# An adaLN attention block on one core: a third row tile is moved behind the first K row, and the scale is made in other parts

## The chip, the core and the metric

The kernel runs on one core of a Trainium2 chip. The core has a matrix engine (PE in the profile, its weight loads PEld), a vector engine (VectorE, DVE), an activation engine (ScalarE, ACT), a general engine (GpSimd, POOL) and a sequencer that issues most transfers (SyncE, SP). The metric is the device time of one execution, in microseconds (us), lower is better. The kernel before took 96.18 us (median of 3 runs, 95.69 to 96.2).

## What is computed

```python
B, N, D = (2, 256, 1152)
mod = (silu(c) @ w_mod).reshape(B, 6, 1, D)
shift_a, scale_a, gate_a = mod[:, 0], mod[:, 1], mod[:, 2]
h = layernorm(x) * (1 + scale_a) + shift_a
q, k, v = split(h @ wqkv, 3)
p = softmax(einsum('bqd,bkd->bqk', q, k) * D ** -0.5)
return x + gate_a * (einsum('bqk,bkd->bqd', p, v) @ wo)
```

All inputs are bfloat16. D is 9 blocks of 128; the 512 token rows (B times N) are 4 row tiles of 128, two for each batch item.

## The kernel before

**How the work is staged.** The row tiles of x are centred, transposed on the matrix engine into `xcT` (9 blocks of D by 512 tokens), and multiplied by 1 + scale block by block, which gives `hTs`. K is made from `hTs` at once, without the layernorm's 1/std, which is multiplied into the scores later, and without the shift, which adds the same to all scores of a query. In the meantime the 1/std of all tokens is made (`rstd_bc`), `normalised` multiplies it into `hTs` to give `hT`, and `shifted` adds the shift. Q and V are made from `hT`, then the scores, softmax, p times V, and the output product.

**K by rows.** K has 9 output blocks f and is summed over 9 blocks k of D, one `wK` row of 288 KB for each k. Five output blocks (NACC) are summed in five PSUM banks (`accs`, the pool MM) as the rows arrive: `k_part(k, tokens)` for the blocks 0 and 1 of D (the part PA; KA is 2), a piece of the tokens at a time, and `k_step(k)` for the rest, with all 512 tokens in one matmul of 128x512 each. For the other four output blocks, the share of the D blocks 0 and 1 is made by `pair` and `pair_part` into a bank `psE` and copied to SBUF by `park` (the `held` tile); the D blocks 2 to 8 are summed by `held_block(i, rows)` in a bank `psK`, and `add_held(i)` adds both.

**Three more PSUM banks.** BA, BB and BC are pools of one bank each. A tile that is put there waits until the one before it in the same bank has been read. Junk matmuls (`fillers`), the transposed tiles `tp`, the scale `psS`, the shift `psH`, `psE`, `psK`, `pT3` and `bc_ps` take turns in them.

**The scale.** `psS` is silu(c) times the scale columns of `w_mod` (`wS`). There are two ways to make it. `scale_rows` uses 128x128 blocks of `wS` as weights and 32 columns of silu(c) as moving operand, 9 matmuls for each block; the result lies as it is needed, and `scale_out` adds 1. `scale_tiles` uses silu(c) as 32 columns of weights in four column tiles of the array and streams `wS`, 36 matmuls for a part; `scale_turned` transposes the result on VectorE (`sT`) and adds 1. The blocks come in the parts PA (2 blocks), PB (3), PC (2) and PD (2). PB is made by `scale_tiles`, the others by `scale_rows`. The shift is made by `shift_tiles` the same way as `scale_tiles`, for all 9 blocks.

**Order.** Every engine's instructions run in the order in which the program records them (`pin`), SP's transfers too. So where a line stands in the code is where its instruction stands on its engine. Transfers go out on SP in the order of L167 to L192 and L532 to L539.

**Lines that the change touches.** The loads L172 to L192; `fillers` L362; the start of the K stage L372 to L419 (tile 2 is transposed at L385 and L386, ahead of the first K row at L395); part PB and the second pairs L420 to L437; the K rows with the parts PC and PD, L453 to L487; the shift L505 to L523. From L557 on (Q, scores, V, output) nothing changes but the line numbers.

Of the kernel before, what the change touches and what calls it, by code (L numbers as in the profile page):

```python
# [16 lines left out]
def kernel(  # L17
# [10 lines left out]
    P = 128  # L28
# [9 lines left out]

    NACC = 5
    NPARK = KT - NACC  # L40
    PA, PB, PC, PD = (0, 2), (2, 5), (5, 7), (7, KT)
    KA = PA[1]
    NR = 32

# [21 lines left out]
    def bank(shape, name, dtype=None, where=None):  # L66
        if where is None:
            where = ring[turn_no[0] % len(ring)]
            turn_no[0] += 1
        return where[0].tile(shape, dtype or F32, tag=where[1], name=name)  # L70
# [36 lines left out]
    def tok(b):  # L107
        return slice(b * N, (b + 1) * N)

    def one(t):  # L110
        return slice(t * P, (t + 1) * P)
# [42 lines left out]
    def load_s(part, k0, k1):  # L154
        load_mod(wS, 1, k0, k1, part[0] * P, part[1] * P)

    def load_k(k0, k1, c0=0, c1=D):
        spq.dma_start(out=wK[:, k0:k1, c0:c1], in_=wqkv_v[:, k0:k1, D + c0 : D + c1])
# [19 lines left out]
    load_s(PB, 4, KT)  # L178
    load_k(2, 3)
    load_k(3, 4)  # L180
    load_k(4, 5)
    load_s(PC, 0, 4)
    load_s(PC, 4, KT)
    load_k(5, 6)
    load_s(PD, 0, 4)
    load_s(PD, 4, KT)
    load_k(6, 7)
    load_k(7, KT)
    for k0, k1 in ((0, 3), (3, 6), (6, KT)):
        load_mod(wH, 0, k0, k1, 0, D)  # L190
    for k0, k1 in ((0, 2), (2, 5), (5, 7)):
        load_q(k0, k1)  # L192

    junk_ps = bank([P, 512], "junk_ps", where=BB)
# [1 line left out]
    def fillers(n):  # L196
        for _ in range(n):
            ten.matmul(junk_ps, lhsT=junk[:, :P], rhs=junk, start=True, stop=True)
# [44 lines left out]
    def centre(t, scalar, op, c0=0, c1=D):  # L243
        vec.tensor_scalar(out=xc[:, t, c0:c1], in0=x_sb[:, t, c0:c1], scalar1=scalar, scalar2=None, op0=op)
# [4 lines left out]
    def transposes(t, h, where):  # L249
        k0, k1 = HALF[h]  # L250
        tp = bank([P, 5, P], "tp", BF16, where)
        for k in range(k0, k1):
            ten.transpose(tp[:, k - k0, :], xc[:, t, k * P : (k + 1) * P], ident)
        tps[t, h] = tp

    def xcT_copy(t, h, on_dve, skip=0):
        k0, k1 = HALF[h]
        dst, srct = xcT[:, k0 + skip : k1, one(t)], tps[t, h][:, skip : k1 - k0, :]
        if on_dve:
            vec.tensor_copy(out=dst, in_=srct)  # L260
        else:
            sca.copy(out=dst, in_=srct)
# [16 lines left out]
    def scale_rows(part, kk0, kk1, js=None, where=None):  # L279
        opened = part == PA  # L280
        if kk0 == 0 and not opened:
            psS[part] = bank([P, part[1] - part[0], NR], "psS", where=where)
        for j0, j1 in [part] if js is None else js:
            for kk in range(kk0, kk1):
                for j in range(j0, j1):
                    ten.matmul(psS[part][:, j - part[0], :], lhsT=wS[:, kk, j * P : (j + 1) * P], rhs=sc_rhs(kk),
                               start=(kk == 0 and j == part[0] and not opened), stop=(kk == KT - 1),
                               skip_group_check=True)
# [5 lines left out]
    wS_v = wS.rearrange("p kk (k j c) -> p kk k j c", k=KT, j=4)  # L294
    sT = const.tile([P, KT, 32], F32)

    def scale_tiles(part, where):
        psS[part] = bank([P, part[1] - part[0], 32], "psS", where=where)
        for kk in range(KT):
            for j in range(4):  # L300
                ten.matmul(psS[part][32 * j : 32 * j + 32], lhsT=sc_rhs(kk), rhs=wS_v[:, kk, part[0] : part[1], j, :],
                           start=(kk == 0), stop=(kk == KT - 1))

    def scale_turned(part):
        vec.transpose(out=sT[:, part[0] : part[1], :].rearrange("p k c -> p (k c)"),
                      in_=psS[part].rearrange("p k c -> p (k c)"))
        vec.tensor_scalar_add(out=s1p[:, part[0] : part[1], :], in0=sT[:, part[0] : part[1], 0:B], scalar1=1.0)
# [4 lines left out]
    def scaled_tp(k, t):  # L312
        vec.tensor_scalar(out=hTs[:, k, one(t)], in0=tps[t, 0][:, k, :], scalar1=s1p[:, k, t // NQ : t // NQ + 1],
                          scalar2=None, op0=ALU.mult)

    def scaled_b(k, b):
        scaled(k, tok(b), s1p[:, k, b : b + 1])
# [4 lines left out]
    def k_part(k, sl):  # L322
        for f in range(NACC):
            ten.matmul(accs[f][:, sl], lhsT=wk(k, f), rhs=hTs[:, k, sl],
                       start=(k == 0 and sl.start == 0), stop=False, skip_group_check=True)

    def pair(i, b, where):
        return bank([P, 2, N], "psE", where=where), NACC + 2 * i, tok(b)

    def pair_part(pr, k):  # L330
        ps, f0, sl = pr
        for i in range(2):
            ten.matmul(ps[:, i, :], lhsT=wk(k, f0 + i), rhs=hTs[:, k, sl],
                       start=(k == 0 and i == 0), stop=(k == KA - 1), skip_group_check=True)
# [6 lines left out]
    def park(pr, on_dve=False):  # L341
        ps, f0, sl = pr
        evac(on_dve, held[:, f0 - NACC : f0 - NACC + 2, sl], ps)

    def k_step(k, f0=0, f1=NACC):
        for f in range(f0, f1):
            ten.matmul(accs[f], lhsT=wk(k, f), rhs=hTs[:, k, :],
                       start=False, stop=(k == KT - 1), skip_group_check=True)
# [10 lines left out]
        vec.tensor_tensor(out=qkT[:, KT + NACC + i, :], in0=psK[i], in1=held[:, i, :], op=ALU.add)  # L359


    fillers(11)  # L362
    scale_open(PA, BA)
    sca.activation(out=e_sb, in_=c_sb, func=ACT.Exp, scale=-1.0)
    gps.tensor_scalar_add(out=e_sb, in0=e_sb, scalar1=1.0)
# [7 lines left out]
    transposes(0, 1, MM)  # L373
    xcT_copy(0, 0, True)
    xcT_copy(0, 1, False)
    transposes(1, 0, MM)
    transposes(1, 1, MM)
    scale_rows(PA, 0, 4)
    centre(2, nmean[:, 2:3], ALU.add)
    xcT_copy(1, 0, True)  # L380
    xcT_copy(1, 1, False)
    scale_rows(PA, 4, KT, js=[(0, 1), (1, 2)])
    scaled(0, tok(0), psS[PA][:, 0, 0:1])
    vec.tensor_copy(out=s1p[:, PA[0] : PA[1], :], in_=psS[PA][:, :, 0:B])
    transposes(2, 0, BB)  # L385
    transposes(2, 1, BC)  # L386
    scaled_tp(0, 2)
    scaled_b(1, 0)
    scaled_tp(1, 2)
    xcT_copy(2, 0, True, skip=KA)  # L390
    xcT_copy(2, 1, False)


    accs = [bank([P, T], "acc", where=MM) for _ in range(NACC)]
    k_part(0, tok(0))  # L395
    k_part(0, one(2))
    pr10 = pair(0, 0, BC)
    pair_part(pr10, 0)
    H3, C3 = 5 * P, 4 * P
    sca.activation(out=xc[:, 3, 0:H3], in_=x_sb[:, 3, 0:H3], func=ACT.Copy, accum_out=ssum[3])  # L400
    half3 = small.tile([P, 1], F32, tag="half3", name="half3")
    vec.reduce_sum(out=half3, in_=x_sb[:, 3, H3:D], axis=AX.X)
    vec.tensor_scalar(out=nmean[:, 3:4], in0=half3, scalar1=ssum[3], scalar2=-1.0 / D, op0=ALU.add, op1=ALU.mult)
    centre(3, nmean[:, 3:4], ALU.add, 0, C3)
    centre(3, nmean[:, 3:4], ALU.add, C3, D)
    k_part(1, tok(0))
    pair_part(pr10, 1)
    k_part(1, one(2))
    pr20 = pair(1, 0, BA)
    park(pr10)  # L410
    pair_part(pr20, 0)
    transposes(3, 0, BB)
    pair_part(pr20, 1)
    transposes(3, 1, BC)
    scaled_tp(0, 3)
    scaled_tp(1, 3)
    xcT_copy(3, 0, True, skip=KA)
# [2 lines left out]
    st3 = small.tile([P, NCH, 6], F32, tag="stats", name="stats")  # L420
    bn_part(3, st3, 0)
    act_var(1)
    k_part(0, one(3))
    scale_tiles(PB, BB)
    k_part(1, one(3))
    scale_turned(PB)
    for k in range(*PB):
        for b in range(B):
            scaled_b(k, b)
    bn_part(3, st3, 1)  # L430
    bn_part(3, st3, 2)
    vec.bn_aggr(out=mvs[:, 3, :], in_=st3)
    pr11, pr21 = pair(0, 1, BA), pair(1, 1, BC)
    for pr in (pr11, pr21):
        for k in range(KA):
            pair_part(pr, k)
        park(pr, on_dve=(pr is pr21))  # L437
    act_var(2)
    parts_sq = const.tile([P, P], BF16)
    gps.memset(parts_sq, 0.0)  # L440
# [16 lines left out]
            for b in range(B):  # L457
                scaled_b(k, b)

    for k in range(*PB):  # L460
        k_step(k)
    held_block(0, (2, 4), BA)
    scale_part(PC)
    held_block(0, (4, 5))
    held_block(1, PB, BC)
    pT3 = bank([P, P], "pT3", BF16, BB)
    ten.transpose(pT3, parts_sq, ident)
    masked = const.tile([P, TT, P], BF16)
    vec.tensor_tensor(out=masked, in0=pT3.unsqueeze(1).to_broadcast([P, TT, P]), in1=mask, op=ALU.mult)
    k_step(5)  # L470
    scale_part(PD)
    k_step(6)
    bc_ps = bank([P, T], "bc_ps", where=BB)
    ten.matmul(bc_ps, lhsT=junk[:, :P], rhs=masked.rearrange("p t n -> p (t n)"), start=True, stop=True)
    held_block(0, PC)
    held_block(1, PC)
    sca.copy(out=rstd_bc, in_=bc_ps)

    def normalised(k):
        vec.tensor_tensor(out=hT[:, k, :], in0=hTs[:, k, :], in1=rstd_bc, op=ALU.mult)  # L480

    for k in range(*PD):
        k_step(k)
    for f in range(NACC):
        evac(False, qkT[:, KT + f, :], accs[f])
# [13 lines left out]
    def shift_tiles(kk0, kk1):  # L499
        for kk in range(kk0, kk1):  # L500
            for j in range(4):
                ten.matmul(psH[32 * j : 32 * j + 32], lhsT=sc_rhs(kk), rhs=wH_v[:, kk, :, j, :],
                           start=(kk == 0), stop=(kk == KT - 1))

    shift_tiles(0, KT)  # L505
    held_block(3, (KA, KT), BC)
    shT = const.tile([P, KT, 32], F32)
    vec.transpose(out=shT.rearrange("p k c -> p (k c)"), in_=psH.rearrange("p k c -> p (k c)"))

    def shifted(i):  # L510
        k, b = divmod(i, B)
        if i % 3 == 2:
            sca.activation(out=hT[:, k, tok(b)], in_=hT[:, k, tok(b)], func=ACT.Identity,
                           bias=shT[:, k, b : b + 1], scale=1.0)
        else:
            vec.tensor_scalar(out=hT[:, k, tok(b)], in0=hT[:, k, tok(b)], scalar1=shT[:, k, b : b + 1],
                              scalar2=None, op0=ALU.add)

    for i in range(KT * B):
        if i in (3 * B, 5 * B):  # L520
            normalised(KT - 2 if i == 3 * B else KT - 1)
        shifted(i)
# [215 lines left out]
```

## Time and profile before

| | us |
|---|---|
| median of 3 runs (lowest, highest) | 96.18 (95.69, 96.2) |
| the profiled execution's own time | 95.85 |
| span of its trace, first to last instruction | 94.1 |
| matrix engine busy | 88.4 (94%) |
| VectorE busy | 70.1 (74%) |
| ScalarE busy | 34.3 (36%) |
| GpSimd busy | 21.1 (22%) |
| granted matrix clock, whole span | 1.00 |

The span is smaller than the execution's time by what lies ahead of the first and behind the last instruction. A busy time counts an instruction from its start to its end; matmuls overlap, and their ends are modelled, so for the matrix engine it is safer to look at the distance between starts: 0.216 us for a 128x512 matmul, 0.109 for 128x256, 0.056 for 128x128, 0.025 for 128x32. All recorded helpers share one line number, L85, so an instruction is told apart by the tiles that it writes and reads: `acc<-hTs,wK` is a K row, `psE` a pair, `psK` a held block, `psQ` the Q product, and `ps` the V, p times V and output products. A row of the timeline merges equal instructions that follow each other on one engine: start, duration, engine, operation, tiles, shape, count, and in square brackets the idle time ahead of it and what ended it.

### The profile page before, as it was taken

What the parts mean: (1) busy time and instruction counts of PE and PEld (TensorE: products, weight loads), DVE (VectorE), ACT (ScalarE), POOL (GpSimd) and SP (SyncE); (2) the same over time, 40 slices, a digit from 0 to 9 for tenths busy, and PEclk for the clock granted to TensorE, in tenths of its full rate; (3) what the DMA queues carried; (4) which work ended last, traced back from release to release, by engine and by line L of the source; (5) the groups of instructions that cost most, each with busy time, mean ns of one, the idle gap of its engine ahead of it and who ended that gap; (6) DMA issues with size and microseconds to landing.
All of it is one profiled execution on the core that took longest, in us unless ns stands there. A gap on an engine that the chain in (4) does not pass through costs nothing.

```text
span 94.1 us, 1693 instructions
## 1 busy us (share of the span) xinstructions
PE 88.4 (94%) x664; PEld 52.6 (56%) x664; DVE 70.1 (74%) x133; ACT 34.3 (36%) x71; POOL 21.1 (22%) x26
## 2 busy tenths in 40 slices
PE   3967999999999999999999999999999999999970
PEld 1346885554445444444469656565679656565660
DVE  2396979256899968999998899990028587889880
ACT  5199789002554600184320688324246300000010
POOL 5623000810000000000000000008999990002000
DMA  2999999999999999999999602200000000302213
GB/s 30 331 302 385 374 394 362 373 410 409 403 409 408 412 409 414 397 373 365 382 412 412 254 8 56 61 2 0 0 0 0 0 0 7 125 37 88 109 47 95
DMA packets 17216, 21.31 MB, mean 226 GB/s; under 512 B 2233, under 2 KB 10553, under 8 KB 17209
## 3 DMA queue, kind: packets, MB, share of 16 engines
q1 hardware_dynamic: 16793, 21.17, 62.0%
q8 instruction: 5, 0.08, 0.4%
q10 hardware_dynamic: 416, 0.04, 0.3%
q14 instruction: 2, 0.02, 0.0%
HBM read 19.76 MB, written 1.18 MB: 223 GB/s over the span
## 4 chain that ended last, share of the span: by engine, by line
PE 84%; DVE 4%; DMA 4%; ACT 2%; SPq 1%; issue 1%; DVEq 0%; ACTq 0%
PE ps L85 39%; PE psQ L85 19%; PE acc L85 11%; PE psK L85 7%; DMA x_sb<-in_x_dram 4%; PE s_ps L85 4%; PE psE L85 2%; DVE o_sb L85 2%; DVE ga L85 2%; PE psS L85 1%; ACT xc L85 1%; SPq L85 1%; PE psH L85 1%; PE tp L85 1%; DVE xc L85 1%
## 5 line engine op out<-in xcount | busy, mean ns | idle before, releaser
L85 POOL PARTITION_ALL_REDUCE gate_bc<-gacc x2 | 13.7, 6886 | 44.6 <-DVE gacc L85 44.6
L85 DVE SCALAR_TENSOR_TENSOR gacc<-wG,scT_f,gacc 128x1152 f32<-128x1152 bf16 x16 | 22.4, 1416 | 0.4
L85 PE MATMUL ps<-wV,hT 128*128 128x384 bf16 x108 | 17.7, 326 | 0.0
L85 PE MATMUL psQ<-hT,wQ 128*128 128x512 bf16 x81 | 17.6, 379 | 0.0
L85 PE MATMUL ps<-wO,attnT 128*128 128x384 bf16 (+3 forms) x108 | 17.2, 322 | 0.0
L85 PEld LDWEIGHTS <-attnT 128*128 128x128 bf16 x117 | 11.1, 98 | 6.5
L85 PEld LDWEIGHTS <-hT 128*128 128x128 bf16 x108 | 10.6, 98 | 6.9
L85 PEld LDWEIGHTS <-wK 128*128 128x128 bf16 x109 | 9.5, 97 | 7.0 <-issue 0.4
L85 PEld LDWEIGHTS <-wQ 128*128 128x128 bf16 x81 | 7.9, 98 | 9.6
L85 PE MATMUL acc<-hTs,wK 128*128 128x512 bf16 (+2 forms) x65 | 11.2, 313 | 0.0
L85 ACT CAST qkT<-psQ 128x512 bf16<-128x512 f32 x9 | 4.9, 597 | 11.1 <-PE psQ L85 11.1
L85 DVE CAST attnT<-ps 128x512 bf16<-128x512 f32 (+1 forms) x6 | 3.5, 603 | 6.8 <-PE ps L85 6.8
L85 DVE TENSOR_TENSOR ga<-ps,gate_bc 128x384 f32<-128x384 f32 (+3 forms) x12 | 6.5, 545 | 2.8 <-PE ps L85 2.7
L85 ACT CAST v_sb<-ps 128x384 bf16<-128x384 f32 x12 | 5.5, 477 | 7.9 <-PE ps L85 7.9
L85 DVE TENSOR_TENSOR o_sb<-ga,x_sb 128x384 bf16<-128x384 f32 (+3 forms) x12 | 6.6, 547 | 0.4
L85 PE MATMUL psK<-hTs,wK 128*128 128x512 bf16 x28 | 6.9, 379 | 0.0
L85 ACT CAST o_sb<-ps 128x128 bf16<-128x128 f32 x1 | 0.3, 266 | 17.3 <-PE ps L85 17.3
L85 DVE TENSOR_TENSOR hT<-hTs,held 128x512 bf16<-128x512 bf16 x9 | 5.7, 685 | 0.9 <-ACT held L85 0.9
L85 PE MATMUL junk_ps<-junk 128*128 128x512 bf16 x11 | 3.9, 527 | 1.5 <-DVE junk L85 1.5
L85 DVE BATCH_NORM_STATS2 stats<-x_sb 128x6 f32<-128x384 bf16 x6 | 3.1, 542 | 2.3 <-DMA x_sb<-in_x_dram 2.3
L85 PE MATMUL s_ps<-qkT 128*128 128x256 bf16 x36 | 4.1, 272 | 0.0
L85 PE MATMUL ps<-pT,v_sb 128*128 128x256 bf16 x36 | 4.1, 272 | 0.0
(82 smaller groups left out, 82.4 us busy)
## 6 DMA issues: line engine op xcount, KB each, us to landing
wH<-in_w_mod_dram SPq DMA_DIRECT2D x3, 864.0 KB, 8.7
wG<-in_w_mod_dram SPq DMA_DIRECT2D x3, 864.0 KB, 13.0
wV<-in_wqkv_dram SPq DMA_DIRECT2D x3, 864.0 KB, 13.5
wO<-in_wo_dram SPq DMA_DIRECT2D x3, 864.0 KB, 9.7
wK<-in_wqkv_dram SPq DMA_DIRECT2D x7, 288.0 KB, 6.9
wQ<-in_wqkv_dram SPq DMA_DIRECT2D x3, 576.0 KB, 12.0
wS<-in_w_mod_dram SPq DMA_DIRECT2D x3, 320.0 KB, 6.5
x_sb<-in_x_dram SPq DMA_DIRECT2D x3, 288.0 KB, 3.4
```

The lines of the kernel that those rows point to most:

```text
L85: r = fn(*a, **k)
```

## The change

The parts of the scale become PA 2, PB 2, PC 2 and PD 3 blocks. PB is now made by `scale_rows`, a block at a time in two banks, and PD by `scale_tiles`, in two pieces with a K matmul between them. Tile 2 is centred, transposed and scaled behind the first K row. The parked pairs, the held blocks and their banks are put in other places, ScalarE takes 768 instead of 640 columns of tile 3's mean, one filler is left out, the loads of K row 4 and of the shift and Q are cut and ordered in another way, the shift product follows the first three matmuls of the last held block, and it is turned in two pieces.

```diff
-    PA, PB, PC, PD = (0, 2), (2, 5), (5, 7), (7, KT)
+    PA, PB, PC, PD = (0, 2), (2, 4), (4, 6), (6, KT)
...
     load_k(3, 4)
-    load_k(4, 5)
     load_s(PC, 0, 4)
     load_s(PC, 4, KT)
+    load_k(4, 5)
     load_k(5, 6)
...
-    for k0, k1 in ((0, 3), (3, 6), (6, KT)):
+    for k0, k1 in ((0, 4), (4, 8), (8, KT)):
         load_mod(wH, 0, k0, k1, 0, D)
-    for k0, k1 in ((0, 2), (2, 5), (5, 7)):
+    for k0, k1 in ((0, 1), (1, 3), (3, 5), (5, 7)):
         load_q(k0, k1)
...
-    def scale_tiles(part, where):
-        psS[part] = bank([P, part[1] - part[0], 32], "psS", where=where)
-        for kk in range(KT):
+    def scale_tiles(part, where, kk0=0, kk1=KT):
+        if kk0 == 0:
+            psS[part] = bank([P, part[1] - part[0], 32], "psS", where=where)
+        for kk in range(kk0, kk1):
...
-    fillers(11)
+    fillers(10)
...
     xcT_copy(0, 1, False)
+    scale_rows(PA, 0, 4)
     transposes(1, 0, MM)
-    transposes(1, 1, MM)
-    scale_rows(PA, 0, 4)
-    centre(2, nmean[:, 2:3], ALU.add)
+    transposes(1, 1, BC)
     xcT_copy(1, 0, True)
     xcT_copy(1, 1, False)
     scale_rows(PA, 4, KT, js=[(0, 1), (1, 2)])
     scaled(0, tok(0), psS[PA][:, 0, 0:1])
     vec.tensor_copy(out=s1p[:, PA[0] : PA[1], :], in_=psS[PA][:, :, 0:B])
+    accs = [bank([P, T], "acc", where=MM) for _ in range(NACC)]
+    k_part(0, tok(0))
+    pr10 = pair(0, 0, BA)
+    pair_part(pr10, 0)
+    centre(2, nmean[:, 2:3], ALU.add)
+    scaled_b(1, 0)
     transposes(2, 0, BB)
     transposes(2, 1, BC)
     scaled_tp(0, 2)
-    scaled_b(1, 0)
     scaled_tp(1, 2)
     xcT_copy(2, 0, True, skip=KA)
-    xcT_copy(2, 1, False)
-    accs = [bank([P, T], "acc", where=MM) for _ in range(NACC)]
-    k_part(0, tok(0))
     k_part(0, one(2))
-    pr10 = pair(0, 0, BC)
-    pair_part(pr10, 0)
-    H3, C3 = 5 * P, 4 * P
+    H3, C3 = 6 * P, 4 * P
...
     centre(3, nmean[:, 3:4], ALU.add, C3, D)
+    xcT_copy(2, 1, False)
     k_part(1, tok(0))
     pair_part(pr10, 1)
     k_part(1, one(2))
-    pr20 = pair(1, 0, BA)
     park(pr10)
+    pr20 = pair(1, 0, BC)
     pair_part(pr20, 0)
     transposes(3, 0, BB)
     pair_part(pr20, 1)
-    transposes(3, 1, BC)
+    transposes(3, 1, BA)
...
-    k_part(0, one(3))
-    scale_tiles(PB, BB)
-    k_part(1, one(3))
-    scale_turned(PB)
-    for k in range(*PB):
-        for b in range(B):
-            scaled_b(k, b)
+    PB1, PB2 = (PB[0], PB[0] + 1), (PB[0] + 1, PB[1])
+    for k in range(KA):
+        k_part(k, one(3))
+    scale_rows(PB1, 0, KT, where=BB)
+    scale_rows(PB2, 0, KT, where=BC)
+    for part in (PB1, PB2):
+        scale_out(part)
+        for k in range(*part):
+            for b in range(B):
+                scaled_b(k, b)
+    pr11 = pair(0, 1, BA)
+    for k in range(KA):
+        pair_part(pr11, k)
+    park(pr11)
+    pr21 = pair(1, 1, BB)
+    for k in range(KA):
+        pair_part(pr21, k)
     bn_part(3, st3, 1)
     bn_part(3, st3, 2)
     vec.bn_aggr(out=mvs[:, 3, :], in_=st3)
-    pr11, pr21 = pair(0, 1, BA), pair(1, 1, BC)
-    for pr in (pr11, pr21):
-        for k in range(KA):
-            pair_part(pr, k)
-        park(pr, on_dve=(pr is pr21))
+    park(pr21, on_dve=True)
...
-    for k in range(*PB):
-        k_step(k)
-    held_block(0, (2, 4), BA)
+    k_step(2)
+    k_step(3, 0, 3)
     scale_part(PC)
+    k_step(3, 3, NACC)
+    held_block(0, PB, BA)
+    held_block(1, PB, BC)
+    k_step(4)
     held_block(0, (4, 5))
-    held_block(1, PB, BC)
+    held_block(1, (4, 5))
+    k_step(5, 0, 2)
+    scale_tiles(PD, BB, 0, 4)
+    k_step(5, 2, 3)
+    scale_tiles(PD, None, 4, KT)
+    k_step(5, 3, NACC)
+    held_block(0, (5, 6))
+    held_block(1, (5, 6))
+    scale_turned(PD)
+    for b in range(B):
+        scaled_b(PD[0], b)
     pT3 = bank([P, P], "pT3", BF16, BB)
     ten.transpose(pT3, parts_sq, ident)
...
-    k_step(5)
-    scale_part(PD)
+    for k in range(PD[0] + 1, KT):
+        for b in range(B):
+            scaled_b(k, b)
     k_step(6)
     bc_ps = bank([P, T], "bc_ps", where=BB)
...
-    held_block(0, PC)
-    held_block(1, PC)
     sca.copy(out=rstd_bc, in_=bc_ps)
...
-    for k in range(*PD):
+    for k in range(7, KT):
         k_step(k)
...
+    held_block(3, (KA, KA + 3), BC)
     shift_tiles(0, KT)
-    held_block(3, (KA, KT), BC)
+    held_block(3, (KA + 3, KT))
     shT = const.tile([P, KT, 32], F32)
-    vec.transpose(out=shT.rearrange("p k c -> p (k c)"), in_=psH.rearrange("p k c -> p (k c)"))
+    def shift_turned(k0, k1):
+        vec.transpose(out=shT[:, k0:k1, :].rearrange("p k c -> p (k c)"),
+                      in_=psH[:, k0:k1, :].rearrange("p k c -> p (k c)"))
...
-        if i % 3 == 2:
+        if i % 3 == 1:
             sca.activation(out=hT[:, k, tok(b)], in_=hT[:, k, tok(b)], func=ACT.Identity,
...
+    shift_turned(0, 3)
     for i in range(KT * B):
+        if i == B:
+            shift_turned(3, KT)
```

`held_block(0, PD)` and `held_block(1, PD)` (L486 and L487) stay where they are, and with the new PD they cover three blocks each instead of two.

## The prediction

> **What bounds the kernel now.** I read the slices of the page first, then the chain of waits in order of time, then the timelines of the matrix engine and VectorE between 6 and 31 us, and last the landings of single transfers. The slices (busy tenths of 2.35 us each):
>
> ```profile
> PE   3967999999999999999999999999999999999970
> ```
>
> From the fifth slice to the last but two the matrix engine is full. The chain of waits (start, duration, what) says the same:
>
> ```profile
> 8.80 0.30 DVE hTs L85
> 9.10 0.04 issue
> 9.14 0.98 PE acc L85 x10
> ...
> 30.66 17.48 PE psQ L85 x81
> 48.14 3.93 PE s_ps L85 x36
> 52.07 36.36 PE ps L85 x234
> ```
>
> VectorE's first scaled block starts the K stage at 9.14, and from there to the end of the products at 88.43 the chain stays on the matrix engine. Nothing behind Q is edited, and its 351 matmuls take 57.8 us without a stall. So the question is one number: by how much does the first Q matmul, at 30.49, move? The matrix engine's timeline up to there:
>
> ```profile
> 7.29 0.65 PE L85 MATMUL psS<-scT_rep,wS 128*128 128x32 bf16 x18
> 8.42 0.68 PE L85 MATMUL tp<-ident,xc 128*128 128x128 bf16 x9 [0.48 <-DVE xc L85]
> ...
> 12.34 0.44 PE L85 MATMUL acc<-hTs,wK 128*128 128x128 bf16 x5
> 12.73 0.57 PE L85 MATMUL psS<-wS,scT_rep 128*32 128x96 bf16 x36
> 13.23 0.45 PE L85 MATMUL acc<-hTs,wK 128*128 128x128 bf16 x5
> ...
> 27.75 1.29 PE L85 MATMUL psH<-wH,scT_rep 128*32 128x288 bf16 x36
> 28.97 1.69 PE L85 MATMUL psK<-hTs,wK 128*128 128x512 bf16 x7
> 30.49 0.81 PE L85 MATMUL psQ<-hT,wQ 128*128 128x512 bf16 x3
> ```
>
> Only the stretch ahead of 9.14 has idle time of size. From K row 2 at 14.40 to 27.66 there are 56 matmuls of 0.216, `bc_ps` 0.22, the transpose 0.06 and two scale parts by rows at 0.45 each: 13.3 us, which is the stretch itself. There is no slack to win there, only waits to add. VectorE in the stretch that the change reorders:
>
> ```profile
> 13.35 0.28 DVE L85 STREAM_TRANSPOSE sT<-psS 128x96 f32<-128x96 f32 x1 [0.20 <-PE psS L85]
> 13.67 0.16 DVE L85 TENSOR_SCALAR s1p<-sT 128x6 f32<-128x6 f32 x1
> 13.86 1.27 DVE L85 TENSOR_SCALAR hTs<-xcT,s1p 128x256 bf16<-128x256 bf16 x6
> 15.04 1.01 DVE L85 BATCH_NORM_STATS2 stats<-x_sb 128x6 f32<-128x384 bf16 x2
> 16.09 0.23 DVE L85 BATCH_NORM_AGGREGATE mvs<-stats 128x2 f32<-128x18 f32 x1
> 16.24 0.63 DVE L85 COPY held<-psE 128x512 f32<-128x512 f32 x1
> ```
>
> It is full from 13.35 to 16.87, and its last piece reads a PSUM bank (pair `pr21`).
>
> **Start of the K stage (L372 to L397).** The scale rows of PA end at 7.94 in the row above; their second half waits for its load (issued at 3.01, 4.5 to land). That load does not move. The first scaled block needs this and tile 1's copy, no longer tile 2's centring (0.52) ahead of it: it starts at 7.99, takes 0.29, and with a hand-over of 0.05 (9.09 to 9.14 in the trace) the K row starts at 8.33 instead of 9.14. That is a head start of 0.81. But nine transposes, 0.51, now stand behind the row. The row and its pair are 7 matmuls of 0.109: 9.09. The transposes run to 9.60. Tile 2's first scaled block can start when four of them are out: 9.09 + 0.17 + 0.22 for the last one's way + 0.04 = 9.52, takes 0.28, hand-over 0.05: `k_part(0, one(2))` starts at 9.85, after a new idle time of 0.25, and row 1 at 10.13, against 10.18 now. The head start is down to 0.05. Nor could more be kept: row 1's load is issued at 4.67, and
>
> ```profile
> wK<-in_wqkv_dram SPq DMA_DIRECT2D x1, 288.0 KB, 5.3
> ```
>
> it lands 5.3 later, at 10.0.
>
> **Tile 3.** VectorE's queue behind 9.52: three more pieces at 0.20, then the half sum over 384 instead of 512 columns (0.67 less 128 columns at about 1 ns, 0.54), and the unchanged 0.11 + 0.21 + 0.04 to the centring at 11.02, against 11.08. ScalarE's 768 columns cost about 0.10 more than its 640 (1.16 for 1152 and 0.74 for 640), but start at 8.98 instead of 9.72: covered. So the rows of tile 3 come 0.06 earlier, at 12.28. Two `k_part` of 0.28, then PB by rows, 18 matmuls in 0.45 as for PC now: 13.29. The pairs need bank BA, which ScalarE's copy of tile 3 frees at about 13.35: 13.40. Eight matmuls of 0.109, and K row 2 starts at 14.27, against 14.40. This is the gain of the whole edit: 0.13. Now, PB by column tiles holds the engine from the K row's end (12.62) to 13.23, 0.61; PB by rows with the bank wait is 0.56.
>
> **Part PC in bank BB (L463).** PC's rows stand behind 8 K matmuls, 14.27 + 1.73 = 16.00, in the bank of `pr21`, which VectorE copies out last. VectorE's queue: PB's first block is read at 13.27 (rows from 12.84, 0.20 to the last start, 0.18 to its end, 0.05); 0.16 + 0.04; two blocks at 0.20; the same once more with the wait of 0.04, so that the statistics start at 14.45; 0.47 each, aggregate at 15.50, and the copy from 15.65 to 16.28. Compared with now, that is two scaled blocks less and one small add more. PC starts at 16.33: a new wait of 0.33. Behind it in the matrix engine's order is everything.
>
> **Part PD by column tiles, in two pieces (L471).** By rows it is 0.45. By column tiles one block costs 0.50 from its start to the next K matmul (12.73 to 13.23), of which nine groups at 0.043 are 0.39 and 0.11 the way out, and 0.09 the way in (27.66 to 27.75). Two pieces cost the ways twice: 0.39 + 2 x 0.20 = 0.79, so 0.34 more. The bounds: nothing for the second pair of ways (0.59 in all), or 0.16 for every way, the time by which a 128x512 matmul's end lies behind its successor's start (0.38 less 0.22), which gives 1.03. I take the rows' 0.20.
>
> The Trainium skill, on the page "TensorEngine Tiling (Array Packing)", section "Key Properties", states that a change of the tiling mode drains the engine, and this speaks against cutting the part in two. The trace agrees in kind, with 0.09 and 0.11 at a change, less than the 0.16 of a full drain; by full drains the forecast below would be 0.24 higher.
>
> **Block 6 (L472).** VectorE must turn PD (0.28), add 1 (0.16) and scale block 6 twice ahead of `k_step(6)`. From the last group of the tiles at 20.88: 0.21 to its end, 0.05, then 0.28 + 0.04 + 0.16 + 0.04 + 0.20 + 0.28 and 0.05 give 22.19. The matrix engine has 4 matmuls and a transpose in between and is there at 21.95. New wait: 0.24. The other blocks of PD and the mask, 0.4, are done by 23.4, when row 7 comes at 23.48.
>
> **The shift (L505 to L523).** Both orders have the same matmuls. The last group of `psH` is 4 matmuls, 0.86, plus 0.22 ahead of Q instead of 7. From its start: 0.34 until VectorE reads (28.75 to 29.09 in the trace), the first piece of 96 columns 0.28, 0.04, ScalarE's half of block 0 0.51, 0.05: 1.22. New wait: 0.14. The second piece (between 0.28 for 96 and 0.48 for 288 columns) and blocks 1 to 3 fit into Q's 1.08 a block.
>
> **At nothing.** The loads: row 4 moves behind PC's 576 KB, some 1.4 us at 400 GB/s, from 14.6 to 16 or so, and is used at 18.1. The shift's last piece lands at 28.3 in both orders (17.72 + 10.6), and is used at about 30.1. Q's first rows land no later than 29.7, used at 31.3. SP has one transfer more to issue, 1.5 (three take 4.41), ahead of the gate's loads; the gate work on VectorE waits 1.06 for these and ends at 49.9, 0.25 ahead of the scores, which themselves move back. Without that cover it would cost 1.2. The filler goes from a time in which the engine waits for x.
>
> **The sum:** -0.13 + 0.33 + 0.34 + 0.24 + 0.14 = +0.92, so Q starts at 31.41. The profiled execution's 95.85 (span 94.1, and 1.75 around it that doesn't change) becomes 96.77. The median of the runs shown is 0.33 above the profiled execution, so I forecast 97.1.
>
> **Rivals.** *VectorE keeps up.* Three of the terms, 0.71, are races between VectorE and the matrix engine, with 0.33, 0.24 and 0.14 between them. If VectorE's queue runs that much earlier than I place it (from 0.33 on, within a stretch of 3.0 us, it decides), only 0.21 is left: 96.4, not slower than can be measured. For it: it starts from handovers that I took at their full 0.05. Against: its instructions have the same shapes as now, and the same durations. *The head start is kept in part*: were there no wait at 9.85 and row 1's load there, 0.25 more would stay: 96.85. Against: the landing at 10.0. *The clock comes later.* With a filler less the engine is idle for 0.94 ahead of the first transposes, not 0.72. The fillers start 0.43 apart up to 4.4 us and 0.22 from there; were the 36 small matmuls behind 6.26 (1.5) and the K rows up to 9.6 slow like the first ones, about 1 us is lost: 98.1. Against: the granted clock is 1.00 throughout now, with an idle time of 0.48 ahead of 8.42.
>
> **Numbers.** A change within 0.5%, 0.48 us, can't be told from none. The chances: forecast 0.66, VectorE keeps up 0.14, head start in part 0.10, clock 0.04, something unseen 0.06, most of it a gain. Slower by more than 0.5%: the forecast, the head start and the clock, 0.81; same 0.15, faster 0.04. The range runs from just under VectorE's case, 96.3, to 97.6, where PD has full drains (0.24) and the other waits are 0.25 longer together.
>
> **What would show it.** K's first row at 8.3; an idle time of about 0.25 ahead of row 0's tile 2; PC's scale rows idle 0.3 behind VectorE's `held` copy; the two groups of column tiles taking 0.8; a wait of `acc` on VectorE's `hTs` at about 22; Q's first matmul at 31.4. I am wrong if Q starts ahead of 31.0.

## The result and the profile after

The changed kernel took 97.18 us (median of 6 runs, 97.04 to 97.53), the kernel before 96.12 in 6 runs (95.69 to 96.67): 1.06 us slower, ratio 1.0114, 95% interval 1.0078 to 1.0149. The forecast was 97.1. The profiled execution took 97.23, with a span of 95.4. Ratios here and below compare means of runs, without single runs that lie more than 1.5% above the fastest of the same kernel (two in all: 98.45 us in `y2_new_start` and 99.52 us in `z2_after_row0_later`).

The chain of waits of the changed kernel, in order of time (start, duration, what; `issue` is time in which the engine waited for nothing that the profile shows):

```profile
3.55 5.22 DMA wK<-in_wqkv_dram
8.77 0.05 issue
8.82 0.72 PE acc L85 x5
...
10.02 0.30 DVE hTs L85
...
16.13 0.56 DVE held L85
16.68 0.04 issue
16.73 0.60 PE psS L85 x18
...
22.07 0.49 DVE hTs L85 x2
22.57 0.04 issue
22.61 1.24 PE acc L85 x5
...
53.40 36.36 PE ps L85 x234
```

Before, the chain stayed on the matrix engine from 9.14 on. Now it starts with row 0's load, and behind the first K row it goes over VectorE three times: at 10.0 for tile 2's first scaled block, at 16.1 for the copy of `held`, and at 22.1 for the scaled block 6. The products at the end take the same 36.36 us. The matrix engine's timeline of the same run:

```profile
8.82 0.72 PE L85 MATMUL acc<-hTs,wK 128*128 128x256 bf16 x5 [0.55 <-DMA wK<-in_wqkv_dram]
...
9.59 0.67 PE L85 MATMUL tp<-ident,xc 128*128 128x128 bf16 x9
10.35 0.99 PE L85 MATMUL acc<-hTs,wK 128*128 128x128 bf16 x10
...
14.67 1.89 PE L85 MATMUL acc<-hTs,wK 128*128 128x512 bf16 x7
16.73 0.60 PE L85 MATMUL psS<-scT_rep,wS 128*128 128x32 bf16 x18 [0.17 <-DVE held L85]
...
19.98 0.59 PE L85 MATMUL acc<-hTs,wK 128*128 128x512 bf16 x2
20.50 0.35 PE L85 MATMUL psS<-wS,scT_rep 128*32 128x96 bf16 x16
21.11 0.40 PE L85 MATMUL psS<-wS,scT_rep 128*32 128x96 bf16 x20 [0.25 <-issue]
21.44 0.61 PE L85 MATMUL acc<-hTs,wK 128*128 128x512 bf16 x2
...
22.31 0.22 PE L85 MATMUL pT<-ident,parts_sq 128*128 128x128 bf16 x1
22.61 1.24 PE L85 MATMUL acc<-hTs,wK 128*128 128x512 bf16 x5
...
30.82 1.04 PE L85 MATMUL psK<-hTs,wK 128*128 128x512 bf16 x4
31.82 1.45 PE L85 MATMUL psQ<-hT,wQ 128*128 128x512 bf16 x5
```

How to read it: a matmul's record ends 0.16 us behind the time at which the next one can start, so the idle time that the row states (0.17 at 16.73) is shorter than the lost time. Row 2 and three matmuls of row 3 start at 14.67 and fill 8 x 0.216 (one record is missing), so the engine was free at 16.40 and lost 0.33. The idle 0.25 at 21.11 stands where the record of one matmul between the two pieces is missing; it is no wait. Q starts at 31.82 instead of 30.49. In the kernel before, K row 2 starts here:

```profile
14.40 3.40 PE L85 MATMUL acc<-hTs,wK 128*128 128x512 bf16 x15
```

One split makes the rest easy. The time from K row 2 to the first Q matmul does not depend on when the loads of the first 10 us land, and the start of K row 2 holds all that does.

| run | K row 0 starts | K row 2 starts | row 2 to Q | against changed |
|---|---|---|---|---|
| before | 9.14 | 14.40 | 16.09 | -1.06 |
| changed | 8.82 | 14.67 | 17.15 | |
| changed, again | 8.41 | 14.25 | 17.14 | -0.01 |

The four terms that the forecast placed behind row 2 (0.33, 0.34, 0.24, 0.14) make 1.05; the trace has 1.06. From Q's first matmul to the first one of the V product it is 21.41 in both kernels (30.49 to 51.90, 31.82 to 53.23 in the timelines), so what the forecast put at nothing behind Q cost nothing.

### The profile page after: what moved, and what is told of

Its sections match the earlier page's. It is cut to its first block, busy times and chain, and to the rows that moved or that the text cites. A ratio compares the mean times of both kernels' runs of the same rounds, so it can differ in the third digit from the quotient of the medians.

```text
span 95.4 us, 1686 instructions
## 1 busy us (share of the span) xinstructions
PE 88.8 (93%) x658; PEld 52.6 (55%) x663; DVE 70.0 (73%) x135; ACT 34.4 (36%) x71; POOL 20.7 (22%) x26
## 4 chain that ended last, share of the span: by engine, by line
PE 80%; DVE 8%; DMA 5%; SPq 3%; issue 1%
PE ps L85 38%; PE psQ L85 18%; PE acc L85 8%; PE psK L85 6%; DMA wK<-in_wqkv_dram 5%; PE s_ps L85 4%; SPq L85 3%; DVE hTs L85 2%; DVE o_sb L85 2%; PE psS L85 2%; DVE ga L85 2%; PE psH L85 1%; DVE stats L85 1%; PE psE L85 1%; PE tp L85 1%
## 5 line engine op out<-in xcount | busy, mean ns | idle before, releaser
L85 ACT ACTIVATE hT<-hT,shT 128x256 bf16<-128x256 bf16 x6 | 2.6, 498 | 4.2 <-DVE shT L85 3.3
```

The costliest lines, as they stand in the source:

```text
L85: r = fn(*a, **k)
```

## The experiments

The eleven kernels were measured in three groups (`after_again`, `e1`, `e2` and `e3`; `y1`, `y2`, `z1` and `z2`; `e5`, `z3` and `f1`). Those of one group shared their runs of the kernel before, so ratios are used where kernels of different groups are compared. "Row 2 to Q" is read from each run's timeline as above.

**The changed kernel again** (`after_again`), without an edit.

> The changed kernel once more, for a second profile and the same chip's times. Theory of the forecast: 1.0 us over the kernel before. If the late landing of K row 0's load (8.77) was chance, it lands near 8.2 here and the K row starts near 8.4; if it comes with this change, it lands near 8.8 again.

Measured: 96.89 us, ratio 1.0092 (1.0054 to 1.0129). Its timeline of the matrix engine:

```profile
8.41 0.71 PE L85 MATMUL acc<-hTs,wK 128*128 128x256 bf16 x5 [0.38 <-DVE hTs L85]
...
14.25 1.89 PE L85 MATMUL acc<-hTs,wK 128*128 128x512 bf16 x8
16.30 0.60 PE L85 MATMUL psS<-scT_rep,wS 128*128 128x32 bf16 x18 [0.16 <-DVE held L85]
...
22.18 1.24 PE L85 MATMUL acc<-hTs,wK 128*128 128x512 bf16 x5
...
31.39 1.89 PE L85 MATMUL psQ<-hT,wQ 128*128 128x512 bf16 x8
```

Here row 0's load took 4.7 us to land instead of 5.2, and it is VectorE that starts the K row. Row 2 at 14.25 and Q at 31.39 are the forecast's 14.27 and 31.41. So the late load of the first profile does not come with every execution of the changed kernel.

**Part PC's bank** (`e1_park_first`).

```diff
+    park(pr21, on_dve=True)
     bn_part(3, st3, 1)
     bn_part(3, st3, 2)
     vec.bn_aggr(out=mvs[:, 3, :], in_=st3)
-    park(pr21, on_dve=True)
```

> The changed kernel, with VectorE's copy of pair pr21 out of bank BB put ahead of tile 3's last two statistics instead of behind them; all else as changed. Theory of the forecast: part PC's scale rows wait 0.33 us for that copy (seen as 16.40 to 16.73 in the profile after), so the kernel loses this wait: -0.33 us, some 96.85 against 97.18, and PC's rows follow the K matmuls without idle time. Rival: the wait only moves, since the copy now delays the statistics and with them 1/std, or the next wait takes its place: 0 to -0.1 us.

Measured: 96.61 us, ratio 1.0053 (1.0029 to 1.0076), against 1.0092 for the changed kernel in the same group. Row 2 to Q is 16.82, 0.33 less. The wait is gone:

```profile
14.31 1.89 PE L85 MATMUL acc<-hTs,wK 128*128 128x512 bf16 x8
16.04 0.60 PE L85 MATMUL psS<-scT_rep,wS 128*128 128x32 bf16 x18
```

Eight matmuls from 14.31 end their turn at 16.04, and PC's rows start there. Nothing took the place of the wait: the rival falls.

**PD in one piece** (`e2_one_piece`).

```diff
-    scale_tiles(PD, BB, 0, 4)
-    k_step(5, 2, 3)
-    scale_tiles(PD, None, 4, KT)
-    k_step(5, 3, NACC)
+    scale_tiles(PD, BB)
+    scale_turned(PD)
+    k_step(5, 2, NACC)
     held_block(0, (5, 6))
     held_block(1, (5, 6))
-    scale_turned(PD)
```

> The changed kernel, with part PD's column tiles in one piece where the first piece stood, and turned at once; all else as changed. Theory of the forecast: a second way into and out of column tiles costs 0.20 us, and block 6 is then ready ahead of its K step, so the wait of 0.24 goes too: -0.44 us, 96.75. Rival: the second piece of PD's load isn't there yet when all nine groups stand together, and the engine waits for it: 0 us or slower.

Measured: 96.53 us, ratio 1.0039 (1.0016 to 1.0063). Row 2 to Q is 16.70, 0.45 less, as expected. In its timeline nine groups stand together and the K row of block 6 no longer waits:

```profile
20.57 0.57 PE L85 MATMUL psS<-wS,scT_rep 128*32 128x96 bf16 x36
21.06 0.82 PE L85 MATMUL acc<-hTs,wK 128*128 128x512 bf16 x3
...
22.15 0.22 PE L85 MATMUL pT<-ident,parts_sq 128*128 128x128 bf16 x1
22.23 1.24 PE L85 MATMUL acc<-hTs,wK 128*128 128x512 bf16 x5
```

All nine groups and the way out take 0.49, and behind the transpose the K row follows after 0.08. The load was there; the rival falls. (The profiled execution is one of those with a late load at the start.)

**PD in three pieces** (`e5_three_pieces`), the same cost in a larger dose: pieces of three groups, with one K matmul between each two.

> The changed kernel with PD's column tiles in three pieces of three groups, a K matmul between each two. Theory: a third way in and out costs 0.20 us on the matrix engine, and the last piece then stands one K matmul nearer to block 6's K step, so that the wait there grows from 0.24 to 0.45: +0.42 us against the changed kernel, ratio to the kernel before about 1.014, and the trace shows the wait at 0.45. Rival: the ways overlap with the K matmuls between the pieces and only the wait grows: +0.2 us.

Measured: 97.64 us, ratio 1.0157 (1.0132 to 1.0182). Row 2 to Q is 17.58, 0.43 more than in the changed kernel:

```profile
20.52 0.31 PE L85 MATMUL psS<-wS,scT_rep 128*32 128x96 bf16 x12
20.76 0.39 PE L85 MATMUL acc<-hTs,wK 128*128 128x512 bf16 x1
21.08 0.31 PE L85 MATMUL psS<-wS,scT_rep 128*32 128x96 bf16 x12
21.32 0.39 PE L85 MATMUL acc<-hTs,wK 128*128 128x512 bf16 x1
...
22.55 0.22 PE L85 MATMUL pT<-ident,parts_sq 128*128 128x128 bf16 x1
23.05 0.38 PE L85 MATMUL acc<-hTs,wK 128*128 128x512 bf16 x1 [0.29 <-DVE hTs L85]
```

From one piece to the next, 20.52 to 21.08, there are 0.56, of which three groups are 0.13 and the K matmul 0.22: each piece pays 0.21 to come and go. And block 6's K row is due at 22.61, behind the transpose, and starts at 23.05: the wait has grown to 0.44.

**Three edits taken back together** (`y1_three_undone`): the edits of `e1_park_first` and `e2_one_piece`, and

```diff
-    held_block(3, (KA, KA + 3), BC)
+    held_block(3, (KA, KA + 2), BC)
     shift_tiles(0, KT)
-    held_block(3, (KA + 3, KT))
+    held_block(3, (KA + 2, KT))
```

> The changed kernel with three edits taken back at once: pr21 copied ahead of the statistics, PD's column tiles in one piece, and the shift product after two instead of three matmuls of the last held block, so that five stand between it and Q. Theory: the losses add up, -0.33 - 0.44 - 0.14 = -0.91 us against the changed kernel, so the time is that of the kernel before (ratio 1.000, within 0.3%), with Q's first matmul at 30.5 where the K row starts at 8.4. Rival: the waits stand in for each other, and one that is taken away comes back later; the gain is then that of the largest alone, about 0.45 us, ratio 1.005.

Measured: 96.32 us against 96.21, ratio 1.0014 (0.9986 to 1.0043). Row 2 to Q is 16.26, 0.89 less than in the changed kernel and 0.17 more than before. The terms add up, and Q follows the last held matmul without a wait. It is as fast as the kernel before, and no faster: 0.14 of the 0.17 is PD, whose three blocks by column tiles in one piece cost 0.59, where its two blocks by rows cost 0.45 before. No version here beats the kernel before by more than can be told.

**The start alone.** `e3_old_start` is the changed kernel with the kernel before's start (L381 to L405, with the first pair in bank BA); `y2_new_start` is the kernel before with the new one.

> The changed kernel, with the start of the K stage as before (tile 2 centred, transposed and scaled ahead of the first K row, 640 columns of tile 3 on ScalarE); all else as changed. Theory of the forecast: the new start is worth 0.05 us at K row 2, so this is 97.2, the same. Rival, from the profile after: the new start has no room behind the load of K row 0 (landed at 8.77 there, and the row started at 8.82 instead of 8.33), so it loses 0.3 to 0.4 us, and the old start gives it back: 96.8.

> The kernel before with the new start of the K stage alone (tile 2 behind the first K row, 768 columns of tile 3 on ScalarE, the banks of the pairs that go with it). Theory of the forecast: the head start of 0.8 us is eaten by the nine transposes and a wait, and 0.05 to 0.1 us is left: ratio 0.999 to 1.000. Rival: the head start survives in a kernel without the other waits: -0.4 us or more, ratio 0.996 or less.

Measured: `e3_old_start` 96.84 us beside 96.89 for the changed kernel in the same group; ratio 1.0081 (1.0051 to 1.011). Its row 2 starts at 14.25, to the hundredth where `after_again` has it, though its row 0 starts at 9.07 instead of 8.41. `y2_new_start` has the ratio 0.9991 (0.9961 to 1.0021). So in the changed kernel a head start of 0.66 at row 0 is worth nothing at row 2. For the kernel before only the ratio speaks, which leaves room for 0.4 us of gain or 0.2 of loss: the profile of `y2_new_start` fell on an execution with late loads (row 0 at 9.29, row 2 at 15.20) and shows no head start. The absolute figures in the first expectation were set against the 97.18 of the result, so they don't tell the theories apart; the run of the changed kernel in the same group does.

**How much room row 0's load has.** In both kernels the loads of row 0 and of tile 3 of x were swapped:

```diff
-    load_k(0, 1)
     load_x(3)
+    load_k(0, 1)
```

> The kernel before with the loads of K row 0 and of x's tile 3 swapped, so that row 0 lands some 0.8 us later (8.9 to 9.1 instead of 8.2). Theory: the old start, at 9.14, hides that: 0 to +0.1 us. Rival: the load counts in both kernels: +0.5 us.

> The changed kernel with the same swap of loads. Theory: the new start has 0.1 us of room behind that load, so the K row starts 0.5 to 0.7 us later and so does Q: +0.4 to +0.6 us against the changed kernel (ratio to the kernel before 1.014 to 1.017). Rival: tile 3's earlier landing, or the wait of tile 2 that stands behind the row anyway, gives it back: 0 to +0.1 us.

Measured: `z1_before_row0_later` 96.31 us, ratio 1.0011 (0.9982 to 1.004), no difference that can be told, though in its profiled execution row 0's load landed at 9.7, row 0 started only at 9.78, and row 2 and Q came 0.52 later than in the profile of the kernel before (14.92 and 31.01): the old start has room for the load, but not without end. `z2_after_row0_later` 98.49 us, ratio 1.0218 (1.0158 to 1.0278): 1.0 to 1.2 us behind the changed kernel by the ratios, twice the expectation. Three of its six executions, the profiled one among them, had a granted clock of 0.980 to 0.983 and took 98.89 to 99.52 us; the other three, at 0.997 to 1.00, took 97.67 to 98.09, which is about what was expected. The timeline of the profiled execution and its clock by windows (columns: window, its length, matmul, weight load, VectorE, ScalarE, GpSimd busy, granted clock, DMA share, GB/s):

```profile
7.67 0.42 PE L85 MATMUL psS<-scT_rep,wS 128*128 128x32 bf16 x10
9.45 1.25 PE L85 MATMUL acc<-hTs,wK 128*128 128x256 bf16 x5 [1.36 <-DMA wK<-in_wqkv_dram]
10.49 0.63 PE L85 MATMUL psE<-hTs,wK 128*128 128x256 bf16 x2
```

```profile
8.00:9.00 1.00, 0.09 (x4) 0.00 (x0) 0.87 (x4) 1.00 (x3) 0.50 (x2) 1.00 0.98 360
9.00:10.00 1.00, 0.55 (x3) 0.43 (x4) 0.11 (x1) 0.89 (x3) 0.00 (x0) 0.68 1.07 335
10.00:11.00 1.00, 1.00 (x7) 0.69 (x6) 0.00 (x0) 0.00 (x0) 0.00 (x0) 0.50 1.07 316
11.00:12.00 1.00, 1.00 (x12) 1.00 (x11) 0.41 (x3) 0.00 (x0) 0.00 (x0) 0.50 1.09 399
12.00:13.00 1.00, 1.00 (x10) 0.89 (x9) 0.89 (x4) 0.69 (x1) 0.00 (x0) 0.61 1.04 367
13.00:14.00 1.00, 1.00 (x15) 0.93 (x14) 0.69 (x3) 0.44 (x1) 0.00 (x0) 1.00 1.15 347
```

The K row starts 1.04 later than in `after_again`, and just ahead of it the granted clock falls to half: its five matmuls of 128x256 take 0.21 each instead of 0.109. From row 0 to row 2 it takes 7.15 instead of 5.84, 1.31 for the clock alone. Row 2 to Q is 17.15 again.

**The same with the clock kept** (`z3_row0_later_filled`): four junk matmuls behind PA's scale rows.

> The changed kernel with the loads of K row 0 and tile 3 of x swapped, as in z2_after_row0_later, and four junk matmuls (0.9 us) in the idle time ahead of the K row. Theory: there the late load cost about 0.6 us and the fall of the granted clock to half (9.37 to 12.78) another 1.2 us in the executions where it falls; the junk matmuls keep the clock, so this runs at 97.5 to 97.8, with the clock at 1.00 from 6 to 14 us. Rival: the load alone costs it all, or the junk matmuls stand in the way: 98.4 as before, or slower.

Measured: 97.34 us in four runs that lie within 0.13, ratio 1.0136 (1.0112 to 1.016), 0.16 below the range expected. The granted clock is 1.00 in its profile from 6 to 14 us, and row 0 to row 2 is back at 5.86. So filling an idle time with useless matmuls made this kernel some 0.8 us faster by the ratios, and row 0 to row 2, 7.15 against 5.86, separates the clock's share from the load's. (The whole times don't: in this profile row 0's load took 4.7 us to land, in the one of `z2_after_row0_later` 5.3.)

**The changed kernel with the idle time filled** (`f1_after_filled`): `fillers(2)` at the same place.

> The changed kernel with two junk matmuls (0.43 us) in the idle time between the scale rows and the first K row (0.55 to 0.6 us). Theory: the changed kernel's own clock does not fall there, so nothing changes: 97.0, ratio to the kernel before 1.009 to 1.011. Rival: part of the loss of the changed kernel is executions in which the granted clock falls behind that idle time, as in z2_after_row0_later; then this is 0.2 to 0.5 us faster.

Measured: 96.93 us, ratio 1.0091 (1.0067 to 1.0115). So no part of the changed kernel's loss that can be told comes from that idle time. The forecast's rival of the clock had it come late, ahead of the first transposes; it falls too, since all six runs of the result have a granted clock of 1.00. The clock's fall in the kernel with swapped loads is another mechanism, at another place.

| run | row 2 to Q | against changed | expected |
|---|---|---|---|
| e1_park_first | 16.82 | -0.33 | -0.33 |
| e2_one_piece | 16.70 | -0.45 | -0.44 |
| e5_three_pieces | 17.58 | +0.43 | +0.42 |
| y1_three_undone | 16.26 | -0.89 | -0.91 |
| e3_old_start | 17.15 | 0.00 | 0 |
| y2_new_start | 16.09 | -1.06 | -1.05 |

The expectations of the last two named only times or ratios; 0 and -1.05 are what the forecast's terms give for them.

## Why the prediction was right

The four waits and prices behind row 2 came out one by one as forecast. That the median came within 0.1 of 97.1 is in part luck: the forecast put the profiled execution at 96.77 and added 0.33, because the median before lay that much above its profiled execution. The changed kernel's profiled execution, 97.23, lay at its median, and its start was 0.40 later than forecast. The two about cancel.

**PC's bank, 0.33.** 16.40 to 16.73 in the first profile, 15.98 to 16.30 in the second; gone when the copy went ahead of the statistics. Shown.

**PD by column tiles in two pieces, 0.34.** The two groups with their ways take 0.81 (20.41 to 21.44, less one K matmul), against 0.79, so 0.36 more than by rows. The price of a change of mode, 0.20 for in and out, held at one, two and three pieces. The full drain of 0.16 each way, the upper bound, did not show.

**Block 6, 0.24.** The engine was free at 22.37 and started at 22.61; 0.44 where the piece stood a matmul and a change of mode later; nothing where it stood earlier. Shown in both directions.

**The shift, 0.14.** Four matmuls from 30.82 end their turn at 31.68, and Q starts at 31.82. It was taken away only together with the other two, where the sum fits.

**The start, -0.13.** The mechanism was right: row 0 came earlier (by 0.7 in the second profile), `k_part(0, one(2))` waited 0.25 for tile 2 (from 9.59 + 0.51 to 10.35 in the first), and nothing of the head start was left at row 2. The term was mis-sized by as much as a load's landing varies. The forecast took two loads from one execution, row 0's (landed at 8.2, needed at 8.33) and the second half of part PA's scale columns (4.5 to land), and put no price on later ones. Where row 0's load takes 4.6 to 4.7 us to land, row 2 starts at 14.25 to 14.31, as forecast. In six of the eight profiles of the new start with the loads in this order it took 5.2 to 5.5 us, and row 2 started at 14.67 or later: 0.4 in the first profile, +0.27 instead of -0.13. In three of these six (`e2_one_piece`, `f1_after_filled`, `y2_new_start`) it was not row 0's load that started the row but VectorE: the scale columns had taken 5.0 to 5.4 us, so its first scaled block was late too. Whether the old start loses as much in such executions stays open, since neither of its two profiles with the loads in this order had a late load. By an estimate from the same rows, a landing after 5.2 to 5.5 us (8.8 to 9.1) is still in time for the old start, which needs the load at 9.09; late scale columns aren't in this estimate. Over all runs the two starts can't be told apart.

**VectorE keeps up**, the rival of 96.4, fell: VectorE's pieces took what the rows of before said, and the three races ended at 0.33, 0.24 and 0.14. **The head start kept in part** asked for row 1's load to be there and for no wait at tile 2. In the second profile that load has landed by 9.8, 0.4 ahead of row 1, and the wait stands all the same: it fell.

## What to carry to other kernels

Where one engine has no idle time left, an edit that only reorders its work can win nothing there, and each place where it now meets a slower engine's queue has a price that can be worked out as a race: the work it has until then against the other queue up to the piece it needs. Put the copy that frees a PSUM bank ahead of work that nobody waits for, and don't cut a block of column tiles in two. Before an edit moves a stage's start up to a load's landing, look at how that landing varies between executions: the time saved at the start was room.

## What the runs showed that was not expected

The granted clock can fall within a kernel that is busy on average. In `z2_after_row0_later` the mean clock of 0.68 in the window from 9 to 10 and 0.61 from 12 to 13 put the fall at 9.36 and the return at 12.78, 3.4 us apart. The matrix engine had been idle for some 1.8 us of the 3.4 ahead of it, 1.44 of them in one piece (from 7.67 + 0.25 on), and otherwise ran almost only transposes and matmuls of 32 columns. The Trainium skill, on the page "TensorE: Matmul & The Clock Gate", in its part on the HAM clock gate, states that the clock falls after an idle window of about 3.4 us: the stretch at half clock has that length here, but ahead of the fall the engine never stood still for 3.4 us: 1.44 at a time was enough. Whether the page's window counts transposes and narrow matmuls as work, this trace doesn't show. In the changed kernel, with 0.5 to 0.7 us idle at the same place, neither profile shows a fall, nor does `e5_three_pieces` with 1.15 us idle there; the changed kernel's slowest single run, 97.8 us, had a granted clock of 1.00. But one of the twelve executions of `y2_new_start`, with the loads in their usual order, took 98.45 us at a granted clock of 0.982, as low as in three of those of `z2_after_row0_later`. It has no profile, so where its clock fell stays open.

The same load, issued at the same time behind the same 1440 KB, landed after 4.6 to 4.7 us in four profiles and 5.2 to 5.5 us in six, with nothing in between. The six are all of kernels with the new start, but so are two of the four, and up to this load nothing is issued in another order; whether that is more than chance, the runs don't show.
